# A windowed attention feeding a leaky feed-forward block: the weights' loads moved to directly behind the first values, and two casts moved between engines

## The chip, the cores and the metric

The kernel runs on one core of a Trainium2 chip. The core has a matrix engine (TensorE, PE in the profile), a vector engine (VectorE, DVE), an engine for functions of single elements (ScalarE, ACT), a general one (GpSimd, POOL) and one that only issues transfers here (SyncE, SP). Sixteen DMA engines move the data that SP and POOL ask for. The metric is the device time of one execution in microseconds (us), lower is better, as the median of several runs.

## The reference

`q`, `k` and `v` have 8 batches, 8 heads, 576 tokens and 64 channels per head. Every token attends to the tokens at most 32 places away:

```python
scores = (1 / sqrt(64)) * (q @ k.transpose(0, 1, 3, 2))
mask   = abs(pos[:, None] - pos[None, :]) <= 32
attn   = softmax(where(mask, scores, -1e9))
x      = (attn @ v).transpose(0, 2, 1, 3).reshape(4608, 512)
h      = x @ w_in                      # 512 -> 2048
out    = maximum(0.01 * h, h) @ w_out  # 2048 -> 512, float32
```

Inputs and outputs are float32. The kernel multiplies in bfloat16.

## The kernel before, in words

Heads go in pairs, four pairs to a batch; the two heads of a pair fill the 128 partitions. The first two batches (0 and 1) are treated in half sequences of 288 tokens, one "step" for each batch, half and pair; the later batches in blocks. For a step of batches 0 and 1 there are these pieces:

- `load_qk(b, p)` (L69) issues on SP one DMA for the queries and one for the keys of a pair, in float32. With `behind` given it has POOL first write one element of the target, so that SP's DMA waits until POOL comes to that place in its queue (L76).
- `load_cast_v(b, p)` (L137) issues on POOL two DMAs that load a pair's values and cast them on the way, into `vbd`.
- `cast_qk(b, p, q_eng, k_eng)` (L262) casts the loaded queries and keys to bfloat16, each on a given engine: VectorE or POOL by a copy (L270), ScalarE by an activation (L268). POOL is the default for both.
- `transposes(b)` (L299) is a generator. Each `next` issues the six PE transposes of one pair's queries or keys (L308) and the copy out of PSUM on ScalarE (L316 for queries, L322 for keys).
- `score(i)` (L398) does the score matmuls of step `i` into the one PSUM tile `ps` (L409 for batch 0, L416 for batch 1), the exponential on ScalarE (L421) and the product with the mask (L423), on POOL but for step 0.
- `sums(i)` (L436) sums the masked exponentials with a matmul of ones into the PSUM tile `s` (L447) and takes the reciprocal on VectorE (L452). The pool has one such tile, so the next `sums` waits for that reciprocal.
- `product(i)` (L455) multiplies with the values into the PSUM tile `x` (L463), and `scaled(i)` (L475) multiplies with the reciprocals into `xT` on VectorE (L477). There is one `x` tile as well.

The feed-forward block works on groups of tokens, 288 at first and 256 or 512 later: `h_mms` and `h_tile` (L498, L514) multiply with `w_in`, `o_tile` and `o_pair` (L562, L582) with `w_out`. Both weights stay on the chip as bfloat16. `load_w_in(f0, f1)` and `load_w_out(i)` (L653, L656) each issue on POOL one DMA of 512 KB that casts on the way; there are four of each.

The order of work is written out by hand: the tile framework runs with a manual schedule, and every engine executes its own instructions in the order of the program. Waits between engines, and the semaphores that signal a DMA's landing, are put in by the framework. The lines L660 to L781 hold the start: batch 0's transposes, steps 0 to 7, and the first two groups of the feed-forward block. Batch 1's queries and keys are loaded there (L718), and its transposes come inside group 1 (`second_pair`, L746). Behind that a planner spreads the remaining steps over the feed-forward matmuls by due times (L784 to L859); the change does not touch it.

`keep_busy(t, lo, n)` (L599) issues `n` matmuls of 224 columns whose results nobody reads, into part of a PSUM tile that is in use elsewhere (`ps` or a feed-forward tile).

Numbers of lines are those of the kernel before. In the kernel after, those from L599 to the start of the listing at L660 are 7 higher, and those behind the listing 6 higher.

Of the kernel before, what the change touches and what calls it, by code (L numbers as in the profile page):

```python
# [9 lines left out]
FP32 = mybir.dt.float32  # L10
# [6 lines left out]
def kernel(  # L17
# [15 lines left out]
    nc = tc.nc  # L33
# [7 lines left out]
    NPAIR = H // 2  # L41
# [19 lines left out]
    xps = ctx.enter_context(tc.tile_pool(name="xps", bufs=1, space=PS))  # L61
# [7 lines left out]
    def load_qk(b, p, behind=None):  # L69

        for into, src, name in ((qf, q, "qf"), (kf, k, "kf")):
            t = fload.tile([96, 2, RUN * D], FP32, name=f"{name}{p}")
            if behind is not None:
                behind.memset(t[0:1, 0, 0:1], 0.0)  # L76
                behind = None
            heads = src[b, 2 * p:2 * p + 2]
            if b < BY_DMA:
                nc.sync.dma_start(out=t, in_=heads.rearrange("a (p c) d -> p a (c d)", c=RUN))  # L80
            elif into is qf:
                nc.sync.dma_start(
                    out=t.rearrange("p a (g e) -> p a g e", g=3),
                    in_=heads.rearrange("a (g p c) d -> p a g (c d)", g=3, c=2),
                )
            else:
                nc.sync.dma_start(
                    out=t.rearrange("p a (c d) -> p a c d", d=D),
                    in_=heads.rearrange("a (c p) d -> p a c d", p=96),
                )  # L90
            into[b, p] = t
# [45 lines left out]
    def load_cast_v(b, p, heads=range(2)):  # L137

        for a in heads:
            r = slice(64 * a, 64 * a + 64)  # L140
            nc.gpsimd.dma_start(
                out=vbd[b % 2][r, p, :, r],
                in_=v[b, 2 * p + a].rearrange("(c p) d -> p c d", p=64),
            )
# [8 lines left out]
    ones_bd = const.tile([128, 128], BF16)  # L153
# [91 lines left out]
    ps = scps.tile([128, 1024], FP32)  # L245
# [16 lines left out]
    def cast_qk(b, p, q_eng=nc.gpsimd, k_eng=nc.gpsimd):  # L262
        for eng, src, dst in ((q_eng, qf, qb), (k_eng, kf, kb)):
            if eng is None:
                continue
            to, tok = dst[:, p], src[b, p].rearrange("p a (c d) -> p c a d", d=D)
            if eng is nc.scalar:
                eng.activation(out=to, in_=tok, func=AF.Copy)  # L268
            else:
                eng.tensor_copy(out=to, in_=tok)  # L270
# [74 lines left out]
    def where(i):  # L345
        return i // 8, (i // 4) % 2, i % 4
# [6 lines left out]
    def score_blocks(i):  # L353
        p, bs = i % NPAIR, blocks_of(i)
        n = 2 * 64 * len(bs)
        lo = 512 * (i % 2)
        sc = ps[:, lo:lo + n].rearrange("p (a w c i) -> p a w c i", a=2, c=2, i=32)
        for w, (b, m) in enumerate(bs):
            tok = qz[b % 2][:, p, m // 3].rearrange("p a (c i) -> p a c i", c=2)
            at = 32 * (m % 3)  # L360
            nc.tensor.matmul(  # L361
                sc[:, :, w], kz[b % 2][:, p, 64 * m:64 * m + 128],
                tok[:, :, :, at:at + 32], start=True, stop=True,
            )
        e = attn.tile([128, 2 * HALF], BF16, name="e")
        nc.scalar.activation(out=e[:, 0:n], in_=ps[:, lo:lo + n], func=AF.Exp, scale=scale)  # L366
        pr = prob[:, i % NPROB].rearrange("p n c i -> p (n c i)")[:, 0:n]
        nc.gpsimd.tensor_mul(pr, e[:, 0:n], band.rearrange("p w c i -> p (w c i)")[:, 0:n])  # L368
        probs[i] = pr.rearrange("p (a w i) -> p a w i", a=2, i=64)
# [28 lines left out]
    def score(i, masked_by=nc.gpsimd):  # L398
        if i >= OLD:
            return score_blocks(i)  # L400
        b, hf, p = where(i)
        by_c = qT[b][:, p].rearrange("p (c i) -> p c i", c=2)
        if b == 0:

            for a, n_, m in ((0, 0, 0), (1, 1, 0), (0, 0, 1), (1, 1, 1), (0, 0, 2),
                             (0, 1, 0), (1, 0, 0), (0, 1, 1), (1, 0, 1), (1, 0, 2)):
                blk, i0, n = WIN[hf][n_][m]
                r = slice(64 * a, 64 * a + 64)
                nc.tensor.matmul(  # L409
                    ps_v[r, n_, :, i0:i0 + n], first_keys[p][r, 64 * blk:64 * blk + 64],  # L410
                    by_c[r, :, hf * EVEN + i0:hf * EVEN + i0 + n], start=True, stop=True,
                )
        else:
            for n_, blocks in enumerate(WIN[hf]):
                for blk, i0, n in blocks:
                    nc.tensor.matmul(  # L416
                        ps_v[:, n_, :, i0:i0 + n], kbd[b % 2][:, p, blk],
                        by_c[:, :, hf * EVEN + i0:hf * EVEN + i0 + n], start=True, stop=True,
                    )
        e = attn.tile([128, 2 * HALF], BF16, name="e")  # L420
        nc.scalar.activation(out=e, in_=ps[:, P0:P0 + 2 * HALF], func=AF.Exp, scale=scale)  # L421
        pr = prob[:, i % NPROB]
        masked_by.tensor_mul(  # L423
            pr.rearrange("p n c i -> p (n c i)"), e, mask[hf].rearrange("p n c i -> p (n c i)"),
        )
        probs[i] = [pr, None, None]
# [9 lines left out]
    def sums(i):  # L436

        b, hf, p = where(i)
        pr, both, r = probs[i]
        if r is not None:  # L440
            return
        s = xps.tile([128, 512], FP32, name="s")[:, 0:HALF]
        if both is not None:
            nc.tensor.matmul(s, ones_bd, both, start=True, stop=True)  # L444
        else:
            for n in range(2):
                nc.tensor.matmul(  # L447
                    s, ones_bd, pr[:, n].rearrange("p c i -> p (c i)"),
                    start=(n == 0), stop=(n == 1),
                )  # L450
        r = recip.tile([128, HALF], FP32, name="r")
        nc.vector.reciprocal(r, s)  # L452
        probs[i][2] = r

    def product(i):  # L455

        b, hf, p = where(i)
        pr = probs[i][0]
        x = xps.tile([128, 512], FP32, name="x")[:, 0:HALF]
        x_v = x.rearrange("p (c i) -> p c i", c=2)  # L460
        parts = [(n_, *block) for n_ in range(2) for block in WIN[hf][n_]]
        for n_, blk, i0, n in parts:
            nc.tensor.matmul(  # L463
                x_v[:, :, i0:i0 + n], vbd[b % 2][:, p, blk, :], pr[:, n_, :, i0:i0 + n],
                start=(blk == parts[0][1]), stop=(blk == parts[-1][1]), skip_group_check=True,
            )
        probs[i][1] = x
# [7 lines left out]
    def scaled(i):  # L475
        _, x, r = probs.pop(i)
        nc.vector.tensor_mul(place(i), x, r)  # L477
# [15 lines left out]
    while t0 < new:  # L493
        n = 256 if t0 < 2048 else min(512, new - t0)
# [87 lines left out]
    def o_pair(hook):  # L582

        o = {}
        for j, part in ((0, 0), (0, 1), (0, 2), (1, 0), (1, 1), (1, 2), (0, 3), (1, 3)):
# [8 lines left out]
            if part == 3:  # L594
                o_sb = outp.tile([128, DMODEL], FP32, name="o_sb")
                nc.scalar.activation(out=o_sb, in_=o[j], func=AF.Copy)
                nc.sync.dma_start(out=out[ts(j, 128)], in_=o_sb)

    def keep_busy(t, lo, n):  # L599


        for _ in range(n):
            nc.tensor.matmul(
                t[:, lo:lo + 224], ones_bd, mask[0].rearrange("p n c i -> p (n c i)")[:, 0:224], start=False, stop=False,
                skip_group_check=True,
            )
# [46 lines left out]
    def load_w_in(f0, f1):  # L653
        nc.gpsimd.dma_start(out=w_in_bf[:, :, f0:f1], in_=w_in_r[:, :, f0:f1])

    def load_w_out(i):  # L656
        c = slice(4 * i, 4 * i + 4)
        nc.gpsimd.dma_start(out=w_out_bf[:, c, :], in_=w_out_r[:, c, :])
# [16 lines left out]
    next(first)  # L675
    next(first)
    load_cast_v(0, 3)
    cast_qk(0, 2, nc.vector)
    sums(0)
    score(1)  # L680
    load_w_in(0, 512)
    next(first)
    keep_busy(ps, 0, 2)
    next(first)
    keep_busy(ps, 0, 3)
    cast_qk(0, 3, nc.vector)
    score(2)
    sums(1)
    next(first)
    keep_busy(ps, 0, 3)  # L690
    next(first)
    product(0)
    scaled(0)
    load_w_in(512, 1024)
    sums(2)
    score(3)
    product(1)
    scaled(1)
    load_w_in(1024, 1536)
    keep_busy(ps, 0, 3)  # L700
    score(4)
    load_w_in(1536, 2048)
    h0 = h_first(0)
    h = next(h0)
    product(2)
# [3 lines left out]
    next(h0)  # L709
    score(5)  # L710
    next(h0)
    load_w_out(0)
    product(3)
    next(h0)
    scaled(3)
    load_w_out(1)

    for p in range(NPAIR):  # L718
        load_qk(1, p, nc.gpsimd if p == 0 else None)
    sums(4)  # L720
    next(h0)
    score(6)
# [71 lines left out]
    at, t = {1: 0.0}, 0.0  # L794
# [10 lines left out]
    t = at[2] - LEAD + 1.8  # L805
    while len(due) + 8 < NC:
# [3 lines left out]
        t = until  # L810
# [77 lines left out]
```

## Time and profile before

| | us |
|---|---|
| runs, median of 3 | 314.67 |
| runs, lowest and highest | 314.0, 315.95 |
| profiled execution | 315.61 |
| its span, first to last instruction | 313.9 |

| engine | busy, us |
|---|---|
| PE matmuls | 298.1 |
| PE weight loads (beside the matmuls) | 194.4 |
| VectorE (DVE) | 224.7 |
| POOL | 205.0 |
| ScalarE (ACT) | 202.2 |

The table's busy times are of one profiled execution; its span is what the views of the trace divide, and the profiled execution's own time is 1.7 us above it. In the rows of the trace, L12 is line 12 of the kernel, `out<-in` are the program's names of tiles, and `x6` is a count. A row of the timeline begins with its start and its length in us, and ends with the engine's idle time before it and what released it. A row of waits ends with the us in total, how often, and the longest. A row of the window table has the window, its length, then the busy us of PE, PE weight loads, DVE, ACT and POOL with counts, the granted clock of PE, the busy share of the DMA engines and their GB/s. A row of DMA issues has the size of one and the median us from issue to landing. A busy PE is not a PE at its peak: ends of matmuls are modelled.

### The profile page before, as it was taken

How to read it: one execution, taken by the hardware profiler on the slowest of the kernel's cores; microseconds unless marked ns; L12 is line 12 of the kernel's file. 1: busy time of each engine (PE TensorE's matmuls, PEld its weight loads, DVE VectorE, ACT ScalarE, POOL GpSimd, SP SyncE). 2: the span in 40 equal slices, each digit the busy share in tenths (PEclk: the TensorE clock that was granted, in tenths of full speed). 3: DMA queues.
4: the chain of work that ended last, by engine and by line, in shares of the span. 5: the costliest groups of instructions: out<-in, count | busy, mean ns of one | idle time of the engine just before them, and what ended most of it. 6: DMA issues, size and time to landing. Idle time of an engine off the chain costs nothing.

```text
span 313.9 us, 6723 instructions
## 1 busy us (share of the span) xinstructions
PE 298.1 (95%) x2511; PEld 194.4 (62%) x2540; DVE 224.7 (72%) x299; ACT 202.2 (64%) x418; POOL 205.0 (65%) x258
## 2 busy tenths in 40 slices
PE   2889979999999999999999999999999999999996
PEld 1567855476765858585858585858555555544643
DVE  6788668878669977898799776898679866753000
ACT  6537775274775858686858686767579548842731
POOL 8889789977799889589668357578947622110000
PEclk9999999999999999999999999999999999999999
DMA  7999999998999999989999994796970011011002
GB/s 198 180 166 172 268 250 132 240 187 168 209 219 201 138 277 184 203 173 255 183 186 179 255 199 90 143 230 156 196 137 2 15 68 55 0 36 67 33 25 79
DMA packets 122017, 48.29 MB, mean 154 GB/s; under 512 B 96256, under 2 KB 117504, under 8 KB 121984
## 3 DMA queue, kind: packets, MB, share of 16 engines
q1 hardware_dynamic: 108288, 42.48, 68.1%
q0 software_dynamic: 13696, 5.38, 14.6%
q8 instruction: 20, 0.33, 0.4%
q14 instruction: 13, 0.11, 0.1%
HBM read 36.70 MB, written 9.44 MB: 147 GB/s over the span
## 4 chain that ended last, share of the span: by engine, by line
PE 77%; DMA 10%; DVE 6%; POOL 3%; issue 2%; ACT 1%; SPq 0%; POOLq 0%; DVEq 0%; ACTq 0%
PE mm L574 34%; PE mm L501 33%; DMA kf<-in_k_dram 7%; DVE r L452 4%; PE ps L361 4%; PE s L379 2%; PE x L379 2%; DMA set<-kb 2%; POOL prob L368 1%; DMA set<-in_v_dram 1%; POOL kb L270 1%; PE s L447 1%; PE x L463 1%; DVE xT L477 1%; DVE r L388 1%
## 5 line engine op out<-in xcount | busy, mean ns | idle before, releaser
L501 PE MATMUL mm<-xT,w_in_bf 128*128 128x256 bf16 (+3 forms) x956 | 133.1, 294 | 0.3
L574 PE MATMUL mm<-w_out_bf,gT 128*128 128x512 bf16 (+2 forms) x537 | 122.5, 373 | 1.3
L388 DVE RECIPROCAL r<-r 128x256 f32<-128x256 f32 (+1 forms) x56 | 95.0, 1696 | 38.0 <-ACT r L387 37.5
L501 PEld LDWEIGHTS <-w_in_bf 128*128 128x128 bf16 x960 | 91.4, 98 | 30.2 <-issue 0.3
L368 POOL TENSOR_TENSOR prob<-e,band 128x512 bf16<-128x512 bf16 (+1 forms) x56 | 62.7, 1120 | 58.4 <-ACT e L366 57.2
L574 PEld LDWEIGHTS <-gT 128*128 128x128 bf16 x560 | 52.1, 98 | 54.1
L512 ACT ACTIVATE gT<-mm 128x288 bf16<-128x288 f32 (+2 forms) x112 | 50.2, 476 | 12.4 <-PE mm L501 9.5
L366 ACT ACTIVATE e<-ps 128x512 bf16<-128x512 f32 (+1 forms) x56 | 32.4, 579 | 27.8 <-PE ps L361 26.5
L579 ACT ACTIVATE o_sb<-mm 128x512 f32<-128x512 f32 (+2 forms) x35 | 20.5, 585 | 39.3 <-PE mm L574 39.1
L535 ACT ACTIVATE gT<-mm 128x512 bf16<-128x512 f32 x64 | 35.7, 596 | 5.5 <-PE mm L501 4.2
L452 DVE RECIPROCAL r<-s 128x288 f32<-128x288 f32 x16 | 31.2, 1952 | 4.4 <-PE s L444 2.3
L270 POOL CAST kb<-kf 96x768 bf16<-96x768 f32 x30 | 24.9, 830 | 3.6 <-DMA kf<-in_k_dram 3.2
L392 DVE TENSOR_TENSOR xT<-s,r 64x256 bf16<-64x256 f32 (+1 forms) x56 | 24.3, 434 | 3.6 <-PE ps L361 0.5
L392 DVE TENSOR_TENSOR xT<-x,r 64x256 bf16<-64x256 f32 (+1 forms) x56 | 24.4, 435 | 3.3
L361 PEld LDWEIGHTS <-set 128*128 128x128 bf16 x216 | 16.7, 98 | 9.7 <-DMA set<-kb 0.5
L423 POOL TENSOR_TENSOR prob<-e,mask 128x576 bf16<-128x576 bf16 x15 | 19.4, 1293 | 4.7 <-ACT e L421 4.6
L296 DVE COPY set<-kT 64x576 bf16<-64x576 bf16 x48 | 21.4, 446 | 1.2 <-DMA kT<-qb 0.3
L361 PE MATMUL ps<-set 128*128 128x128 bf16 x216 | 21.4, 219 | 0.3 <-DMA set<-kb 0.3
L275 POOL CAST set<-vbuf 128x640 bf16<-128x640 f32 x24 | 17.2, 718 | 3.8 <-DMA vbuf<-in_v_dram 3.8
L270 POOL CAST qb<-qf 96x768 bf16<-96x768 f32 x24 | 19.7, 820 | 0.0
L379 PEld LDWEIGHTS <-set 128*128 128x128 bf16 x432 | 18.0, 98 | 0.5
L421 ACT ACTIVATE e<-ps 128x576 bf16<-128x576 f32 x16 | 10.4, 651 | 10.2 <-PE ps L409 6.1
(83 smaller groups left out, 241.3 us busy)
## 6 DMA issues: line engine op xcount, KB each, us to landing
qf<-in_q_dram SPq DMA_DIRECT2D x32, 288.0 KB, 5.8
kf<-in_k_dram SPq DMA_DIRECT2D x32, 288.0 KB, 6.3
out_dram<-o_sb SPq DMA_DIRECT2D x35, 256.0 KB, 3.0
vbuf<-in_v_dram SPq DMA_DIRECT2D x15, 256.0 KB, 4.8
w_in_bf<-in_moe_w_in_dram POOLq DMA_DIRECT2D x4, 512.0 KB, 5.7
w_out_bf<-in_moe_w_out_dram POOLq DMA_DIRECT2D x4, 512.0 KB, 14.9
vbuf<-in_v_dram SPq DMA_DIRECT2D x10, 192.0 KB, 4.6
set<-in_v_dram POOLq DMA_DIRECT2D x16, 72.0 KB, 7.0
```

What stands on the lines that cost most here:

```text
L270: eng.tensor_copy(out=to, in_=tok)
L361: nc.tensor.matmul(sc[:, :, w], kz[b % 2][:, p, 64 * m:64 * m + 128], tok[:, :, :, at:at + 32], start=True, stop=True,)
L366: nc.scalar.activation(out=e[:, 0:n], in_=ps[:, lo:lo + n], func=AF.Exp, scale=scale)
L368: nc.gpsimd.tensor_mul(pr, e[:, 0:n], band.rearrange("p w c i -> p (w c i)")[:, 0:n])
L379: nc.tensor.matmul(x[:, a, w], vw[b % 2][:, p, m, a:a + 2].rearrange("p n d -> p (n d)"), pr[:, a, w], start=True, stop=True,)
L388: nc.vector.reciprocal(r[:, 0:n], r[:, 0:n])
L392: nc.vector.tensor_mul(xT[rows, p, t0:t0 + n].rearrange("p (w i c) -> p w c i", i=32, c=2), x[rows, a].rearrange("p (w c i) -> p w c i", c ...
L452: nc.vector.reciprocal(r, s)
L501: nc.tensor.matmul(h[:, 0:n], w_in_bf[:, c, ts(f, 128)], xT[:, c, t0:t0 + n], start=(c == 0), stop=(c == DMC - 1),)
L512: nc.scalar.activation(out=to, in_=h, func=AF.Prelu, alpha=0.01)
L535: nc.scalar.activation(out=gT[:, f - 1:f + 1, t0:t0 + 256], in_=hh.rearrange("p (f t) -> p f t", f=2), func=AF.Prelu, alpha=0.01,)
L574: nc.tensor.matmul(o[:, lo:hi], gT[:, f, t0:t0 + 128], w_out_bf[:, f, lo:hi], start=(f == 0), stop=(f == FFC - 1),)
```

## The change

The weights' loads move ahead in POOL's queue. The first two chunks of `w_in` are issued directly behind batch 0's values, ahead of the mask product of step 1; the third and the fourth follow the products of steps 2 and 3, and `w_out`'s first chunk the product of step 4. Batch 1's queries and keys are loaded ahead of `w_out`'s second chunk, and not behind it. Pair 2's keys are cast on VectorE where POOL cast them; pair 3's queries on ScalarE where VectorE cast them. Three of the `keep_busy` calls become `warm_up` calls: nine matmuls of 128 columns in all for eight of 224, into a PSUM tile of their own (the pool of `x`) and not into `ps`.

```diff
+    def warm_up(n):
+        t = xps.tile([128, 512], FP32, name="x")
+        for _ in range(n):
+            nc.tensor.matmul(
+                t[:, 0:128], ones_bd, ones_bd, start=True, stop=True, skip_group_check=True,
+            )
...
     load_cast_v(0, 3)
-    cast_qk(0, 2, nc.vector)
+    load_w_in(0, 512)
+    load_w_in(512, 1024)
+    cast_qk(0, 2, nc.vector, nc.vector)
     sums(0)
     score(1)
-    load_w_in(0, 512)
     next(first)
-    keep_busy(ps, 0, 2)
+    warm_up(2)
     next(first)
-    keep_busy(ps, 0, 3)
-    cast_qk(0, 3, nc.vector)
+    cast_qk(0, 3, nc.scalar)
+    warm_up(4)
     score(2)
+    load_w_in(1024, 1536)
     sums(1)
     next(first)
-    keep_busy(ps, 0, 3)
+    warm_up(3)
     next(first)
     product(0)
     scaled(0)
-    load_w_in(512, 1024)
     sums(2)
     score(3)
+    load_w_in(1536, 2048)
     product(1)
     scaled(1)
-    load_w_in(1024, 1536)
     keep_busy(ps, 0, 3)
     score(4)
-    load_w_in(1536, 2048)
+    load_w_out(0)
     h0 = h_first(0)
...
     score(5)
     next(h0)
-    load_w_out(0)
+    for p in range(NPAIR):
+        load_qk(1, p, nc.gpsimd if p == 0 else None)
+    load_w_out(1)
     product(3)
     next(h0)
     scaled(3)
-    load_w_out(1)
-
-    for p in range(NPAIR):
-        load_qk(1, p, nc.gpsimd if p == 0 else None)
     sums(4)
```

## The prediction

> **What bounds the kernel now.** I read the page's totals first, then what TensorE (PE) waited for, then the stages.
>
> ```profile
> span 313.9 us, 6723 instructions
> PE 298.1 (95%) x2511; PEld 194.4 (62%) x2540; DVE 224.7 (72%) x299; ACT 202.2 (64%) x418; POOL 205.0 (65%) x258
> ...
> PE tp L308 <- POOL kb L270: 1.9, 2, 1.1
> PE s L447 <- DVE r L452: 1.0, 3, 0.6
> PE ps L361 <- DMA set<-kb: 0.3, 1, 0.3
> ...
> 40.00:45.00 5.00, 3.18 (x40) 2.63 (x41) 2.98 (x7) 3.77 (x9) 4.69 (x7) 1.00 1.17 271
> 50.00:55.00 5.00, 4.80 (x39) 2.66 (x38) 4.75 (x10) 2.68 (x6) 5.00 (x8) 1.00 0.96 143
> 55.00:60.00 5.00, 4.39 (x36) 2.28 (x35) 4.79 (x5) 1.02 (x3) 4.87 (x7) 1.00 1.33 212
> 60.00:70.00 10.00, 9.95 (x87) 7.03 (x86) 6.67 (x10) 6.27 (x15) 7.70 (x10) 1.00 1.21 214
> ```
>
> PE is busy 95% of the span. In the window rows PE's busy time is the second figure: from 60 us on it leaves nothing to speak of (9.95 of 10, and from there to the end one semaphore wait, the 0.3 of L361). So whatever this change does before 60 us passes through to the end as PE's arrival time there, and only two stretches hold idle PE that an edit could win back: 40 to 45 us (1.8 us idle; the two waits of L308 for POOL's cast of keys, 1.9 us) and 50 to 60 us (0.2 + 0.6 us, for DVE's reciprocals). The two together are 2.7 us, under 1% of the span. What comes before 20 us is a chain of single steps that starts the work, and any delay in it moves PE's whole queue.
>
> **POOL's queue, where the weights move to.** The weights' DMAs are issued by POOL, between its own work, in program order.
>
> ```profile
> 4.10 6.21 POOL L141 DMA_DIRECT2D set<-in_v_dram  x8
> 10.63 0.82 POOL L270 CAST kb<-kf 96x768 bf16<-96x768 f32 x1 [0.33 <-DMA kf<-in_k_dram]
> 12.07 1.27 POOL L423 TENSOR_TENSOR prob<-e,mask 128x576 bf16<-128x576 bf16 x1 [0.62 <-ACT e L421]
> 13.51 0.83 POOL L654 DMA_DIRECT2D w_in_bf<-in_moe_w_in_dram  x1 [0.17 <-issue]
> 14.34 0.84 POOL L270 CAST kb<-kf 96x768 bf16<-96x768 f32 x1
> ...
> set<-in_v_dram POOLq DMA_DIRECT2D x1, 72.0 KB, 9.1
> ```
>
> The last row is the first of the eight value loads, taken alone: issued at 4.10, landed 9.1 us later, at 13.2. This matters because in the compiled program POOL's DMAs take eight semaphores in rotation: the ninth, which is the first weights' load, carries a wait for the first value load, the tenth for the second, in both kernels. Before, that wait is free: POOL gets there at 13.51, after its cast and its mask product. After, the two loads stand right behind the eight value loads, so POOL reaches them at 4.10 + 6.21 = 10.31 and waits until 13.2. Queued behind the waiting issue are the mask product of step 1 and the key cast of pair 3. So: issue 13.3, two issues of 0.83 each to 14.95; product of step 1 from 14.95 to 16.2 (before 12.07 to 13.34, **2.9 us later**); cast of pair 3's keys to 17.05 (before 15.18); product of step 2, again 1.27, to 18.3. The DMA queue itself gains little at its head, since the value loads hold it anyway; the second chunk does start earlier, but no wait of PE for a weight is in the list above for it to shorten.
>
> **Who waits for it.** PE takes its instructions in order.
>
> ```profile
> 14.38 0.66 PE L447 MATMUL s<-prob,ones_bd 128*128 128x288 bf16 x2
> 15.08 1.96 DVE L452 RECIPROCAL r<-s 128x288 f32<-128x288 f32 x1 [1.33 <-PE s L447]
> 17.10 0.42 PE L447 MATMUL s<-prob,ones_bd 128*128 128x288 bf16 x2 [0.20 <-DVE r L452]
> 17.55 1.96 DVE L452 RECIPROCAL r<-s 128x288 f32<-128x288 f32 x1 [0.16 <-PE s L447]
> 19.43 0.40 DVE L477 TENSOR_TENSOR xT<-x,r 128x288 bf16<-128x288 f32 x1
> 19.88 0.40 PE L463 MATMUL x<-prob,set 128*128 128x96 bf16 x5 [0.38 <-DVE xT L477]
> 20.84 0.65 PE L501 MATMUL mm<-xT,w_in_bf 128*128 128x288 bf16 x4
> ```
>
> sums(1) (14.38) needs the product of step 1, so it starts at 16.25; its reciprocal at 16.95 instead of 15.08, to 18.9; sums(2) at 19.0 instead of 17.10, and at the slow 0.66 (below) instead of 0.42, so the next reciprocal starts at 19.65 instead of 17.55; scaled(1), product(2) and the first matmul of the feed-forward follow at 21.6, 22.05 and 23.0. **Loss in front: 2.15 us.**
>
> **The casts and the warm-up.**
>
> ```profile
> 12.28 1.48 DVE L270 CAST qb<-qf 96x768 bf16<-96x768 f32 x1
> 13.09 0.65 ACT L322 ACTIVATE kT<-tp 128x576 bf16<-128x576 bf16 x1 [0.52 <-PE tp L308]
> 14.50 0.65 ACT L421 ACTIVATE e<-ps 128x576 bf16<-128x576 f32 x1 [0.77 <-PE ps L409]
> 12.04 0.53 PE L603 MATMUL ps<-mask,ones_bd 128*128 128x224 bf16 x2 [0.16 <-ACT e L421]
> 9.45 0.55 DVE L270 CAST qb<-qf 96x768 bf16<-96x768 f32 x1
> ```
>
> Pair 2's keys go to DVE, which is free from 10.0 to 10.40: at the 0.55 of the cast at 9.45, from the landing at 10.6 to 11.2. The new warm-up writes another PSUM tile, so it doesn't wait for the exponential as the row at 12.04 does; the transposes behind it start near 11.9 instead of after both fillers, 12.4. Pair 3's queries go to ACT: no ACT cast of 96x768 is in the trace, between the 0.65 of 576 columns and the 1.48 that DVE needed; I take 0.85, by the nearer row. It falls into the 0.77 us for which ACT waited before 14.50 anyway. All this wins up to 0.5 us ahead of sums(1) and hands it to PE's wait for POOL: I count it as nothing. Were the stall not there, the cover would be gone and the 0.3 to 0.5 us would count. The 1.48 leaving DVE count nothing either: the reciprocal behind it waited 1.33 us for PE.
>
> **PE's slow start.**
>
> ```profile
> 9.22 0.66 PE L308 MATMUL tp<-ident,kb 96*128 96x96 bf16 x6 [0.80 <-DVE kb L270]
> ...
> PEclk9999999999999999999999999999999999999999
> ```
>
> The page's row of the granted clock reads full from the start and doesn't show it, but the two matmuls of sums(1) take 0.66 at 14.38 and those of sums(2) 0.42 at 17.10, so PE turned fast in between. Before that it had worked since this row's 9.22 with no pause above 0.3 us. In the changed kernel this work is cut by the stall: PE stands from about 13.95 to 16.25, and again near 18.5 and 20.5. Gapless work starts at 22.05. Bounds for the cost: nothing, if PE turns fast by then; at the other end, slow for as long as 9.22 to 16.6 (7.4 us) counted from 22.05, to 29.5, so 6.5 us of feed-forward at about half speed, 3.2 us. I take 0.9, nearer to nothing, since the last, unbroken part of before (13.79 to 16.6) was under 3 us: slow to about 24.8, half of 1.8 us. **PE comes to batch 1's transposes 2.15 + 0.9 = 3.05 us later.**
>
> By the Trainium skill, "TensorE: Matmul & The Clock Gate", Part 1 (the HAM clock gate), the clock opens after about 3.4 us of sustained work, in a free-running window, and an idle window closes it. By that rule the stall starts the count afresh; worst case two windows from 22.05, to 28.9, which would put about 2.9 in place of 0.9, an estimate. The trace agrees in the slow first matmuls; it doesn't show the window.
>
> **Batch 1's queries and keys.**
>
> ```profile
> 25.58 0.09 POOL L76 MEMSET qf<- 1x1 f32 x1
> 25.70 0.31 SPq L80 DMA_DIRECT2D qf<-in_q_dram  x1
> 24.05 1.55 POOL L658 DMA_DIRECT2D w_out_bf<-in_moe_w_out_dram  x2
> w_out_bf<-in_moe_w_out_dram POOLq DMA_DIRECT2D x4, 512.0 KB, 14.9
> 46.08 2.75 PE L590 MATMUL mm<-w_out_bf,gT 128*128 128x512 bf16 x12
> qf<-in_q_dram SPq DMA_DIRECT2D x1, 288.0 KB, 8.8
> qf<-in_q_dram SPq DMA_DIRECT2D x32, 288.0 KB, 5.8
> 40.10 0.82 POOL L270 CAST kb<-kf 96x768 bf16<-96x768 f32 x1 [2.28 <-DMA kf<-in_k_dram]
> 40.98 0.43 PE L308 MATMUL tp<-ident,kb 96*128 96x96 bf16 x6 [1.06 <-POOL kb L270]
> 43.84 0.82 POOL L270 CAST kb<-kf 96x768 bf16<-96x768 f32 x1 [0.21 <-DMA kf<-in_k_dram]
> 44.71 0.43 PE L308 MATMUL tp<-ident,kb 96*128 96x96 bf16 x6 [0.84 <-POOL kb L270]
> ```
>
> SP starts these eight loads after POOL's memset and has nothing else to issue in this stretch. The memset is now one weights' issue (0.8) earlier in POOL's queue; but POOL's product ahead of it follows PE and is 2 to 3 us late, and with the other reorderings I place it near 26.4, 0.8 later than 25.58. In exchange only one chunk of w_out stands ahead, and w_in's second and third are through sooner. The first load took 8.8 us against a median of 5.8 over all: up to 3 us of it was queueing. So landings move by +0.8 to -2.2 us; I take 0, as a shared DMA moves the same bytes. The second chunk of w_out, now issued behind the memset at about 26.5 instead of 24.9, lands some 15 us later by the row, at 41.5, and PE reads it from 46: nothing. Then the casts end at 40.92 and 44.66 as now, and PE, which without its waits would come to the second at 44.71 - 1.9 = 42.8, comes at 42.8 + 3.05 = 45.85. The 1.9 us of waits swallow most of the loss; left is 1.15. Of the 0.8 idle at 50 to 60, DVE's chain behind the last query load stands where it was, so PE gets that back too: left is +0.35.
>
> **Sum:** 2.15 + 0.9 - 1.9 - 0.8 = +0.35 us. The profiled execution took 315.61 (span 313.9 and 1.7 around it), so it would take 316.0; the runs' median is 314.67, 0.94 lower, so I forecast **315.1**, no change.
>
> **Rivals.**
> - The wait hides after all, and the early loads do their work (POOL's stall covered, or value loads landing by 10.3). Against it: 13.2 from the rows above. Then 0.3 in front, 1.5 to 1.9 at 40 to 45, up to 0.8 behind: -2.3, so **312.4**. Chance 0.15.
> - The slower side: PE stays slow through the first feed-forward group because the stall breaks its work. Price 3.2 in place of 0.9; it decides once the loss in front passes 1.9 + 0.8 = 2.7. Sum 2.15 + 3.2 - 2.7 = +2.65: **317.3**. For it: three pauses where there were none. The rule of the Trainium skill named above speaks for it too. Against: dense work from 22 on. Chance 0.15.
> - The change doesn't bring the loads sooner but later (+0.8): the second cast ends at 45.5, DVE's chain and PE with it, and nothing is regained behind: +0.8 to 1.2, **315.7**. Chance 0.2.
> - The loads land 1 to 2 us sooner with PE fast by 23: 2.15 - 2.7 = -0.55: **314.1**. Chance 0.15.
>
> **How the numbers follow.** The forecast has 0.35. Range 312.8 to 317.4: it holds the forecast and its neighbours, most of the slower rival, and a part of the fast one. The measurement tells about 1% (3.1 us) from no change; the three runs alone lie 314.0 to 315.95. A gain above that would need more than all the idle PE that the stages hold (2.7): 0.03. A loss above it needs the slow PE and late loads together: 0.07. Same: 0.90.
>
> **What would show it.** POOL idle from about 10.3 to 13.3, ended by a DMA or "issue", ahead of the first weights' load; sums(1) near 16.2 instead of 14.38; the first feed-forward matmul near 23.0; PE's waits of 1.06 and 0.84 gone at 41 and 45; PE's idle before the reciprocals at 50 to 57 smaller. I am wrong if POOL doesn't stall at 10.3, if the slow matmuls last beyond 25, or if the second key cast ends before 43.5 or after 45.5.

## The result, and the profile after

The changed kernel takes 316.19 us (median; 315.01 to 318.24), the kernel before 314.69 in the same series. The ratio is 1.0052, with a 95% interval of 1.0036 to 1.0067: slower by 1.5 us, inside the 1% that was forecast as no change, and 1.1 us above the forecast of 315.1. The profiled execution took 315.80 with a span of 314.1, so the two profiles alone differ by 0.2 us of span.

The page of the changed kernel, its totals; then the waits of PE over the whole span and of POOL from 5 to 60 us (us in total, times, longest):

```profile
span 314.1 us, 6755 instructions
PE 300.7 (96%) x2541; PEld 195.7 (62%) x2541; DVE 228.3 (73%) x299; ACT 202.2 (64%) x419; POOL 204.7 (65%) x257
...
PE s L447 <- POOL prob L423: 2.2, 1, 2.2
PE s L447 <- DVE r L452: 0.8, 3, 0.3
...
POOL w_in_bf L661 <- DMA set<-in_v_dram: 2.5, 1, 2.5
```

The last row is the wait that the change adds: POOL stands 2.5 us at the first weights' load, until the values' DMA lands. The first row of waits is its price on PE: sums(1) waits 2.2 us for POOL's mask product. PE's two waits for key casts, 1.9 us before, are gone from the list but for a rest too short to show. (The counts of matmuls differ between the two pages because a few records are missing from the first.)

Two rows of the kernel before for comparison, batch 1's first transposes and the `sums` near 56 us:

```profile
36.91 0.42 PE L308 MATMUL tp<-ident,qb 96*128 96x96 bf16 x6
56.10 0.42 PE L447 MATMUL s<-prob,ones_bd 128*128 128x288 bf16 x2 [0.61 <-DVE r L452]
```

The timeline of the changed kernel in the front, then at batch 1's casts and transposes:

```profile
10.04 0.78 DVE L270 CAST kb<-kf 96x768 bf16<-96x768 f32 x1
12.81 0.83 ACT L268 ACTIVATE qb<-qf 96x768 bf16<-96x768 f32 x1
12.89 1.53 POOL L661 DMA_DIRECT2D w_in_bf<-in_moe_w_in_dram  x2 [2.46 <-DMA set<-in_v_dram]
14.49 1.27 POOL L423 TENSOR_TENSOR prob<-e,mask 128x576 bf16<-128x576 bf16 x1
15.81 0.64 PE L447 MATMUL s<-prob,ones_bd 128*128 128x288 bf16 x2 [2.18 <-POOL prob L423]
18.50 0.66 PE L447 MATMUL s<-prob,ones_bd 128*128 128x288 bf16 x2 [0.32 <-DVE r L452]
23.17 0.69 PE L447 MATMUL s<-prob,ones_bd 128*128 128x288 bf16 x2
23.65 0.98 PE L501 MATMUL mm<-xT,w_in_bf 128*128 128x288 bf16 x4
24.56 0.43 PE L409 MATMUL ps<-set,kT 64*64 64x64 bf16 x10
27.06 0.09 POOL L76 MEMSET qf<- 1x1 f32 x1
...
32.80 6.05 POOL L750 MEMSET set<- 128x1152 bf16 x6
40.00 0.42 PE L308 MATMUL tp<-ident,qb 96*128 96x96 bf16 x6
44.78 0.84 POOL L270 CAST kb<-kf 96x768 bf16<-96x768 f32 x1
45.68 0.43 PE L308 MATMUL tp<-ident,kb 96*128 96x96 bf16 x6
56.30 0.42 PE L447 MATMUL s<-prob,ones_bd 128*128 128x288 bf16 x2 [0.23 <-DVE r L452]
```

sums(1) moves from 14.38 to 15.81, sums(2) from 17.10 to 18.50. The two matmuls of a `sums` still take 0.69 at 23.17, and the ten of a score 0.43 at 24.56: PE turns fast only there (at 24.3 by the record of the granted clock in the trace), where it was fast at 17.10 before. The first feed-forward matmul starts at 23.65 (before 20.84), batch 1's first transposes at 40.00 (before 36.91), the transposes behind the second of the key casts at 45.68 (before 44.71), and the `sums` of 56.10 stands at 56.30. So 3.1 us of loss in front are 1.0 us at 45 and 0.2 at 56.

The same in the window table of the changed kernel (PE's busy time is the second figure):

```profile
40.00:45.00 5.00, 5.00 (x62) 4.25 (x60) 4.13 (x9) 4.85 (x13) 4.88 (x8) 1.00 1.20 264
50.00:55.00 5.00, 5.00 (x51) 3.06 (x49) 4.73 (x10) 2.67 (x5) 5.00 (x7) 1.00 0.71 121
55.00:60.00 5.00, 4.77 (x38) 2.43 (x36) 4.79 (x5) 1.56 (x3) 4.87 (x8) 1.00 1.38 215
```

PE's 1.8 us of idle at 40 to 45 are filled, and 0.6 of the 0.8 at 50 to 60. The late PE has used up the slack that the late loads had made, in this pair of profiles.

### The profile page after: what moved, and what is told of

Its sections match the earlier page's. It is cut to its first block, busy times and chain, and to the rows that moved or that the text cites. A ratio compares the mean times of both kernels' runs of the same rounds, so it can differ in the third digit from the quotient of the medians.

```text
span 314.1 us, 6755 instructions
## 1 busy us (share of the span) xinstructions
PE 300.7 (96%) x2541; PEld 195.7 (62%) x2541; DVE 228.3 (73%) x299; ACT 202.2 (64%) x419; POOL 204.7 (65%) x257
## 4 chain that ended last, share of the span: by engine, by line
PE 77%; POOL 11%; DMA 4%; DVE 3%; issue 2%; ACT 2%; SPq 0%; POOLq 0%; ACTq 0%; DVEq 0%
PE mm L574 34%; PE mm L501 33%; PE ps L361 3%; DVE r L452 2%; POOL set L750 2%; PE x L379 2%; PE s L379 2%; POOL kb L270 2%; POOL prob L368 2%; DMA set<-kb 1%; DMA kf<-in_k_dram 1%; POOL prob L423 1%; POOL qb L270 1%; POOL set L141 1%; PE s L447 1%
## 5 line engine op out<-in xcount | busy, mean ns | idle before, releaser
L574 PE MATMUL mm<-w_out_bf,gT 128*128 128x512 bf16 (+2 forms) x560 | 124.6, 373 | 0.0
L392 DVE TENSOR_TENSOR xT<-s,r 64x256 bf16<-64x256 f32 (+1 forms) x56 | 24.3, 434 | 3.6 <-PE ps L361 0.5
L392 DVE TENSOR_TENSOR xT<-x,r 64x256 bf16<-64x256 f32 (+1 forms) x56 | 24.3, 435 | 3.3
L270 POOL CAST kb<-kf 96x768 bf16<-96x768 f32 x29 | 24.3, 838 | 1.4 <-DMA kf<-in_k_dram 0.9
L361 PEld LDWEIGHTS <-set 128*128 128x128 bf16 x216 | 16.8, 98 | 9.7 <-DMA set<-kb 0.4
```

Source lines behind the costliest of these rows:

```text
L361: nc.tensor.matmul(sc[:, :, w], kz[b % 2][:, p, 64 * m:64 * m + 128], tok[:, :, :, at:at + 32], start=True, stop=True,)
L392: nc.vector.tensor_mul(xT[rows, p, t0:t0 + n].rearrange("p (w i c) -> p w c i", i=32, c=2), x[rows, a].rearrange("p (w c i) -> p w c i", c ...
L574: nc.tensor.matmul(o[:, lo:hi], gT[:, f, t0:t0 + 128], w_out_bf[:, f, lo:hi], start=(f == 0), stop=(f == FFC - 1),)
```

## The experiments

The theory at the start: POOL's wait for the first value load delays the mask product of step 1 and with it PE's whole queue; the slow clock adds to it; the waits for key casts and reciprocals give most of it back. The rivals: the shorter fillers and the cast on ScalarE cost the time; or early weights take DMA time from what is needed first.

### The weights back in their places

```diff
 # the changed kernel, with
-    load_w_in(0, 512)        # behind load_cast_v(0, 3)
-    load_w_in(512, 1024)
+    load_w_in(0, 512)        # behind score(1)
+    load_w_in(512, 1024)     # behind scaled(0); the others as before, too
```

> The changed kernel with the six loads of w_in and of w_out's first chunk put back to their places in POOL's queue of before; the casts, the fillers and the order of batch 1's loads stay as changed. Stall theory (the loss comes from POOL waiting at the first weights' load for the first value load to land): POOL's idle of 2.46 us before that load falls below 0.5 us, sums(1) starts near 13.8 instead of 15.8, the first feed-forward matmul near 20.4 instead of 23.65, the two waits for key casts at 41 and 45 us come back in part; time 313.5 to 314.5, 1.7 to 2.7 below the changed kernel. Rival (the fillers of 128 columns and the cast on ScalarE make PE slow for longer): the time stays at 315.5 to 316.5 with the turn of the clock near 24.

Measured: 314.33 us; ratio to the kernel before 0.999 (0.997 to 1.001), against 1.0052 for the whole change. PE's timeline in this kernel:

```profile
13.39 0.66 PE L447 MATMUL s<-prob,ones_bd 128*128 128x288 bf16 x2
20.74 0.65 PE L501 MATMUL mm<-xT,w_in_bf 128*128 128x288 bf16 x4
42.77 0.43 PE L308 MATMUL tp<-ident,kb 96*128 96x96 bf16 x6 [0.35 <-POOL kb L270]
```

sums(1) no longer waits for POOL, and the loss is gone: the weights' places are worth 1.9 us. The rival with the fillers isn't out altogether: sums(1) starts 0.2 to 1.0 us earlier than in three profiles of the kernel before (14.38, 14.15, 13.57), and yet the first feed-forward matmul starts no earlier than there (20.84, 20.60, 20.26). PE's clock turned at 20.2 (by the record of the granted clock) and not at 16.4 to 16.8.

### The same early places, without the wait

```diff
 # the changed kernel, with
-    load_cast_v(0, 3)        # ahead of load_w_in(0, 512)
     load_w_in(0, 512)
     load_w_in(512, 1024)
...
     score(2)
+    load_cast_v(0, 3)
     load_w_in(1024, 1536)
```

> The changed kernel with pair 3's two value loads put behind the mask product of step 2, so that the first two weights' loads are the seventh and eighth DMA of POOL and take semaphores that are free; they stand even earlier in the queue. Stall theory: no wait of POOL before the first weights' load, sums(1) near 13.8, first feed-forward matmul near 20.4, time 312.5 to 314. Rival (early weights themselves cost, by taking DMA time from the values and from batch 1's queries and keys): POOL does not wait, but the time stays above 315.5, with PE waiting for values or for key casts.

Measured: 313.70 us; ratio 0.9971 (0.9948 to 0.9994). POOL's first weights' loads, and PE's first feed-forward matmul:

```profile
8.75 1.55 POOL L661 DMA_DIRECT2D w_in_bf<-in_moe_w_in_dram  x2
21.76 1.04 PE L501 MATMUL mm<-xT,w_in_bf 128*128 128x288 bf16 x4
```

The two loads go out 4 us earlier than in the changed kernel and POOL doesn't wait, though they stand two value loads further ahead. Early weights do no harm; the wait does. It comes from the semaphores: these are now POOL's seventh and eighth DMA, and in the trace they take the last two of POOL's eight semaphores; in the changed kernel they take the first two a second time. The expected start of the feed-forward block near 20.4 was missed by 1.4 us: PE stayed slow to 22.5, with no stall in front of it.

### The stall filled

```diff
 # the changed kernel, with
     score(2)
+    warm_up(20)
     load_w_in(1024, 1536)
     sums(1)
```

> The changed kernel with 20 more filler matmuls of 128 columns ahead of sums(1), about 2 us of PE work in the place where PE waits 2.2 us for POOL. The stall stays. If the slow clock is the second part of the loss, PE turns fast before 20 us instead of at 24.3, the first feed-forward matmul starts near 22.8 instead of 23.65, and the time falls by 0.5 to 1.2 us, to 315.0 to 315.7. If the clock's turn costs nothing that reaches the end, the time stays at 316.2 (plus or minus 0.4).

Measured: 314.77 us; ratio 1.000 (0.998 to 1.002), 1.4 us below the changed kernel. PE in this kernel:

```profile
15.88 0.64 PE L447 MATMUL s<-prob,ones_bd 128*128 128x288 bf16 x2 [0.31 <-POOL prob L423]
18.58 0.42 PE L447 MATMUL s<-prob,ones_bd 128*128 128x288 bf16 x2 [0.90 <-DVE r L452]
22.32 0.65 PE L501 MATMUL mm<-xT,w_in_bf 128*128 128x288 bf16 x4
38.39 0.42 PE L308 MATMUL tp<-ident,qb 96*128 96x96 bf16 x6
```

POOL waits as long as in the changed kernel (2.4 us) and sums(1) starts as late, 15.88 against 15.81. But PE is fast from 16.9, the feed-forward block starts 1.3 us earlier and batch 1's first transposes 1.6 us (38.39 for 40.00), and the kernel is as fast as the one before, 0.2 us below the expected range. So the slow clock behind the stall is worth 1.4 us. That doesn't make the wait itself free: PE still comes to batch 1's transposes 1.5 us later than before (38.39 for 36.91), which the waits for key casts give back (0.2 us is left of 1.9). A kernel without the stall and with a fast PE comes to 312.58 (below).

### The first two loads alone

```diff
 # the kernel before, with
     load_cast_v(0, 3)
+    load_w_in(0, 512)
+    load_w_in(512, 1024)
...
     score(1)
-    load_w_in(0, 512)
...
     scaled(0)
-    load_w_in(512, 1024)
```

> The kernel before with one edit: the first two loads of w_in directly behind the values, all casts, fillers and other loads as before. Stall theory: the cast of pair 2's keys stands behind the waiting load on POOL too, so its transposes start near 15.5 instead of 12.4 and the loss in front is larger than that of the whole change, 3.5 to 5 us at the first feed-forward matmul; the waits at 41 and 45 us give back about 1.9 and those behind 50 about 0.5; time 316 to 317.5. Rival (the weights' places do nothing, the loss is that of the other edits): 314.7, as before.

Measured: 317.90 us; ratio 1.0113 (1.0085 to 1.0142). POOL's wait and PE's wait behind it:

```profile
13.29 1.52 POOL L654 DMA_DIRECT2D w_in_bf<-in_moe_w_in_dram  x2 [2.88 <-DMA set<-in_v_dram]
15.73 0.66 PE L308 MATMUL tp<-ident,kb 96*128 96x96 bf16 x6 [3.16 <-POOL kb L270]
24.18 0.65 PE L501 MATMUL mm<-xT,w_in_bf 128*128 128x288 bf16 x4
47.22 0.43 PE L308 MATMUL tp<-ident,kb 96*128 96x96 bf16 x6 [1.09 <-POOL kb L270]
```

It lies 0.4 above the expected range. The front is nearly as expected: pair 2's key cast stands behind POOL's wait, and the first feed-forward matmul is 3.3 us later, where 3.5 to 5 was expected. The clock turned at 19.9, ahead of the feed-forward block, so this loss is the stall's and the late keys', without a slow feed-forward. The waits for batch 1's keys don't give it back, because the weights that follow move POOL's memset, and the key loads behind it, to 28.9: PE waits at 47 again. In the whole change two other edits would soften the first: the cast on VectorE takes the keys out of POOL's queue, and the loads' new place ahead of a weights' issue keeps them from going as late (the memset at 27.06).

### Batch 1's loads alone

```diff
 # the kernel before, with
     load_w_out(0)
+    for p in range(NPAIR):
+        load_qk(1, p, nc.gpsimd if p == 0 else None)
+    load_w_out(1)
     product(3)
     next(h0)
     scaled(3)
-    load_w_out(1)
-
-    for p in range(NPAIR):
-        load_qk(1, p, nc.gpsimd if p == 0 else None)
```

> The kernel before with one edit: batch 1's queries and keys issued ahead of w_out's second chunk. If this part does something by itself, SP's first load starts 0.8 us earlier (near 24.9), PE's two waits for key casts (1.06 and 0.84 us) shrink together by 0.8 to 1.6 us and the time falls by as much less what the reciprocals at 50 to 57 us set: 313.7 to 314.4. If a shared DMA only deals the same bytes out in another order, the waits stay within 0.4 us of 1.9 and the time is 314.7.

Measured: 313.77 us; ratio 0.9967 (0.9951 to 0.9982): this part alone is faster by 1.0 us. POOL's memset, the landing of batch 1's four key loads (the last figure is the median us from issue to landing), batch 1's first transposes, the cast that waits for a key load, and PE's one wait for a key cast:

```profile
25.34 0.09 POOL L76 MEMSET qf<- 1x1 f32 x1
...
kf<-in_k_dram SPq DMA_DIRECT2D x4, 288.0 KB, 12.2
...
37.45 0.42 PE L308 MATMUL tp<-ident,qb 96*128 96x96 bf16 x6
39.21 0.82 POOL L270 CAST kb<-kf 96x768 bf16<-96x768 f32 x1 [0.78 <-DMA kf<-in_k_dram]
43.81 0.43 PE L308 MATMUL tp<-ident,kb 96*128 96x96 bf16 x6 [0.75 <-POOL kb L270]
```

Of 1.9 us of waits 0.75 are left. The memset isn't 0.8 earlier as expected (25.34 against 25.58), and with one chunk of weights less ahead the keys land 12.2 us after they are issued, against 14.2 and 13.3 in the first two profiles of the kernel before. But the cast that waits for them starts at 39.21, and in three profiles of the kernel before at 40.10, 39.20 and 39.75. Against the second of these nothing is gained at the transposes behind the second key cast (43.80 there, behind a wait of 0.83), and PE waits less here also because it comes later (37.45 for 36.91, 36.68 and 36.34). That this part is faster is shown by the times, and the second branch of the expectation, a time of 314.7, is out; by which way it gains, this one profile doesn't show.

### A fast PE from the start

The 38 fillers fill PE's idle time up to 11 us. They were put into the kernel before, into the changed kernel and into that with the values last.

```diff
     load_cast_v(0, 1)
+    warm_up(16)
     next(first)
     next(first)
+    warm_up(8)
...
     score(0, masked_by=nc.vector)
+    warm_up(3)
     next(first)
+    warm_up(8)
     next(first)
...
     sums(0)
+    warm_up(3)
     score(1)
```

> The kernel before with 38 more filler matmuls of 128 columns in the places where PE idles before 11 us (16 ahead of the first transposes, then 8, 3, 8 and 3). If PE's slow start is a matter of its own activity, PE turns fast before 11 us instead of at 16.6, the first feed-forward matmul starts 0.5 to 1.5 us earlier than 20.84, and the time falls less than that, by 0 to 0.8 us, to 313.9 to 314.7, since the key casts at 41 and 45 us then hold PE.

> The changed kernel with the same 38 fillers. The stall of POOL stays (2.4 us); what PE's slow clock adds to it is taken away. If the median's loss of 1.5 us is the clock's, this kernel comes to 314.0 to 315.0, at most 0.5 above the kernel before with the same fillers. If it is the stall's own, it stays 1.2 or more above that kernel, at 315.5 or more.

> The kernel with pair 3's value loads put last (no stall) and the same 38 fillers: a fast PE from 11 us on and no wait of POOL. Theory: first feed-forward matmul near 19.5 to 20, time 312.0 to 313.3, below both kernels. Rival (whatever is won in front is held again by batch 1's key casts at 41 and 45): PE waits there again by 1 us or more and the time stays at 313.7 or above.

Measured: the kernel before with them 314.45 us, ratio 0.9979 (0.9960 to 0.9999); the changed kernel with them 315.82, ratio 1.0029 (1.0012 to 1.0046); the values last with them **312.58, ratio 0.9920 (0.9903 to 0.9937)**, below both kernels, and 1.1 below the same kernel without the fillers. The clock turned at 11.8, 9.9 and 14.0. What I expected of the front didn't come: the first feed-forward matmul starts at 20.64 in the kernel before with fillers (0.5 to 1.5 earlier than 20.84 was expected) and at 20.86 with the values last (19.5 to 20).

The changed kernel stays 1.4 us above the kernel before with the same fillers, which I had put down as the mark of a stall that costs by itself. The trace shows that it can't be read so: the fillers didn't take the slow clock away. The window table of the changed kernel with fillers (PE's busy time is the second figure, the granted clock the third from the end):

```profile
9.90:13.20 3.30, 2.20 (x41) 1.73 (x39) 2.80 (x3) 2.37 (x6) 0.88 (x2) 1.00 1.92 188
13.20:16.60 3.40, 1.31 (x24) 1.10 (x25) 0.44 (x1) 1.49 (x4) 3.33 (x5) 1.00 1.84 168
16.70:20.00 3.30, 2.60 (x28) 1.60 (x25) 2.86 (x3) 1.48 (x3) 1.73 (x2) 0.50 1.23 201
20.00:23.40 3.40, 3.16 (x26) 2.27 (x26) 1.60 (x3) 0.84 (x2) 3.03 (x3) 0.50 1.08 155
23.60:27.00 3.40, 3.26 (x43) 2.13 (x41) 3.29 (x3) 1.19 (x3) 2.56 (x5) 1.00 1.24 157
```

PE is fast from 9.9. In the stretch of the stall it works 1.31 of 3.4 us, and from 16.7 on it is granted half the clock, to 23.4: longer than the stall lasted, and nearly as late as in the changed kernel without fillers (24.3). So the stall closes the clock anew, though PE was fast before. It isn't this execution alone: in all twelve the mean granted clock of the span is 0.984 to 0.989, and two stretches of 3.4 us at half speed make 0.989. The Trainium skill, "TensorE: Matmul & The Clock Gate", Part 1, gives a free-running window of about 3.4 us, after which a busy PE is granted the full clock and an idle one half. The stretches agree with that length (6.8 us at half speed here, 3.4 below); the closing here needed no idle window, a pause of 2.0 us in one was enough.

The kernel before with fillers shows the same at another place, in its window table:

```profile
42.00:45.90 3.90, 1.90 (x21) 1.25 (x20) 1.47 (x4) 2.18 (x5) 2.59 (x5) 1.00 1.23 253
46.00:49.30 3.30, 3.30 (x14) 1.34 (x12) 3.04 (x5) 1.81 (x2) 3.30 (x5) 0.50 1.93 132
49.40:52.00 2.60, 2.60 (x24) 1.49 (x22) 2.19 (x8) 0.92 (x2) 2.60 (x5) 1.00 0.16 29
```

PE didn't wait for the first of the key casts, came to the second one earlier (42.38 where it came at 43.45), waited 1.9 us for it, and ran the next 3.4 us at half speed. What was won was not only held up at the cast, it was paid for with clock. In this kernel that is the exception: of its eleven executions two have a mean granted clock under 0.999, 0.995 for this one and 0.989, and they are the two longest (315.73 and 315.68; the others 313.11 to 314.97).

With the values last and the loads ahead neither pause is there, and PE is fast from 14 on:

```profile
20.86 0.65 PE L501 MATMUL mm<-xT,w_in_bf 128*128 128x288 bf16 x4
24.42 0.09 POOL L76 MEMSET qf<- 1x1 f32 x1
36.96 0.42 PE L308 MATMUL tp<-ident,qb 96*128 96x96 bf16 x6
42.64 0.43 PE L308 MATMUL tp<-ident,kb 96*128 96x96 bf16 x6
```

The feed-forward block and batch 1's first transposes stand where they stood before (20.84, 36.91). The gain is made behind: POOL comes to the memset 1.2 us earlier, the keys are cast in time, and the transposes behind the second key cast stand at 42.64 for 44.71.

### More profiles of both kernels

> The kernel before once more, for a second profile. Its first profiled execution took 315.61, 0.9 above the median of its runs. If the turn of PE's clock differs from one execution to the next and makes that difference, this one turns at another time than 16.6, or falls back to the slow clock behind the waits at 41 and 45 us, and its span follows: about half a us of span for each us of slow clock that falls into the feed-forward stage. If the turn stays at 16.6 within 0.5 and the span still differs by 0.8 or more, the spread has another cause.

> As the second profile of the kernel before: a third sample of the turn of PE's clock, of the two waits for key casts near 41 and 45 us, and of the span. Spans without a slow stretch in the feed-forward stage should lie at 312.5 to 313.3.

> The changed kernel once more. Its first profile turned at 24.3, had its first feed-forward matmul at 23.65 and a span of 314.1, below the median of its runs less 1.7 (314.5). The stall is fixed by the values' landing, so POOL's wait of 2.2 to 2.6 us and sums(1) near 15.8 should be the same; what differs is the turn of the clock (17 to 28) and with it the first feed-forward matmul (23 to 24.5) and the span (313.5 to 316.5).

> As the second profile of the changed kernel: a third sample of the turn of PE's clock and of the span. If the stall sends PE back to the slow clock each time, no sample turns for good before 19.5, and the mean span of the three lies 1 to 2 us above that of the three of the kernel before.

Measured: the kernel before 314.47 and 314.80, spans 312.8 and 313.1; the changed kernel 315.68 and 315.38, spans 313.9 and 313.7. With the first profiles the spans average 313.25 before and 313.91 after: 0.66 apart, where 1 to 2 was expected. The clock turned at 16.4 and 16.8 before (first profile 16.6), and at 23.6 and 24.8 after (first 24.3): it isn't the turn that made the first profile of the kernel before the longest of the three. POOL's wait in the changed kernel was 2.98 and 2.22 us (2.2 to 2.6 expected), and in the first of these two sums(1) started at 16.24. PE's timeline of the second profile of the kernel before, and POOL's first weights' load in it:

```profile
13.68 0.83 POOL L654 DMA_DIRECT2D w_in_bf<-in_moe_w_in_dram  x1 [0.57 <-DMA set<-in_v_dram]
40.08 0.43 PE L308 MATMUL tp<-ident,kb 96*128 96x96 bf16 x6 [0.51 <-POOL kb L270]
43.80 0.43 PE L308 MATMUL tp<-ident,kb 96*128 96x96 bf16 x6 [0.83 <-POOL kb L270]
```

The two key transposes stand 0.9 us earlier than the 40.98 and 44.71 of the profile that the prediction was made from; in the third profile they stand between, at 40.63 and 44.34. In the first, batch 1's keys had landed late. Its waits for key casts (1.9 us in all) are not larger than in the others (1.3 and 2.1), but its PE stands latest at the `sums` of 56.10 (55.19 and 55.74). The first row shows, in the kernel before, the very wait that the prediction took from the list of semaphores: this time POOL reached the load 0.57 us before the value load had landed.

## Why the prediction was right, and where it was off

- **POOL's wait.** Right: it stood from 10.43 (8.93 + 1.50, the end of the value loads' issue) to 12.89 where 10.3 to 13.3 was forecast, named as a wait for the value load. The mask product stood at 14.49 (forecast 14.95), sums(1) at 15.81 (16.25).
- **The casts and fillers.** Right to cost nothing beside the stall: ScalarE took 0.83 (I took 0.85), VectorE 0.78 (0.55). That the new fillers are weaker than the old I hadn't weighed; in the two kernels with the new ones and without the stall the clock turned at 20.2 and 22.5, and behind a stall it turned at 19.9 with the old ones (the first two loads alone) and at 23.6 to 24.8 with the new. Whether the fillers or the windows' place made that, no run here separates. By the time, casts and fillers together are what the kernel with the weights back (0.999) and that with batch 1's loads alone (0.9967) differ in: 0.2%, with intervals that overlap.
- **The slow clock.** Mechanism right, size wrong. The term was 0.9 us, for feed-forward work at half speed to 24.8; the clock turned at 24.3. With the stall filled PE came to batch 1's transposes at 38.39 instead of 40.00: 1.6 us for the slow clock. I left out that the steps between the stall and the feed-forward block go at half speed as well. By the time, filling the stall is worth 1.4 us.
- **Front in sum.** 3.05 us later at batch 1's transposes was forecast, 3.09 measured, and that is luck: the slow clock took 1.6 where I had 0.9, the rest of the front 1.5 (38.39 against 36.91, with the stall filled) where I had 2.15.
- **The loads.** Their issue came at 27.06 where 26.4 was forecast. No landing decided: the second key cast, at 44.78, started behind POOL's own queue (memsets to 38.85, two casts, value loads, a memset) with no idle time. Forecast for the transposes behind it: 45.85; measured 45.68. But I had left the casts where they were, the second one to 44.66; it ends at 45.62 (45.55 and 45.43 in the two other profiles), past the 45.5 that I had named as a sign of being wrong in two of the three. It costs little only because PE comes about as late.
- **What comes back.** 1.9 us at 40 to 45 and 0.8 at 50 to 60 were forecast, from 3.05 to 0.35; measured from 3.09 to 0.2. In the pair of profiles the sum held. What I named for the second part, the chain behind the last query load, isn't what the chain of work that ended last goes through in these two: that is a value load of batch 1, which landed at 49.36 before and 49.56 after.
- **From the profile to the median: here the forecast was off.** It was 316.0 for the profiled execution of the changed kernel, which took 315.80. I then took 0.94 us off, since the profiled execution of the kernel before stood that much above the median, as if both kernels shared it. They don't: the changed kernel's stood 0.39 below its median. In the kernel before it came at least in part from keys whose casts started 0.4 to 0.9 us later than in the two other profiles, and the changed kernel has that slack eaten by its late PE. Against the second profile, with 42.5 for PE's arrival without its waits (43.80 less the 1.3), the same working gives 45.55 and about +1.0 us at the end: 313.8 by its span of 312.8. Against the third (44.34 and 2.1) it gives about +0.2, 313.3 by its span of 313.1. The three spans after are 313.7 to 314.1.
- **What stays open.** The medians differ by 1.5 us and the mean spans of three profiles by 0.66, so more than half of the loss is seen in no profile. None of the profiled executions is one of the longest of the changed kernel (up to 318.24). A clock that closes again later isn't the reason: the mean granted clock is 0.999 or 1.000 in all 22 executions.
- **The rivals.** "The change doesn't bring the loads sooner but later" is nearest by the time (315.7) and had the end of the second cast right (45.5), though POOL's queue made it and not a landing, and PE did regain most of it behind. "The clock stays slow" had the right mechanism at twice its price (3.2 for 1.6). "The wait hides" is out. "The loads land sooner" is borne out for the loads alone only by the time (1.0 us); here POOL's queue came in its place.

## What to carry to other kernels

Before a DMA is moved forward in an engine's queue, count which semaphore it takes: the ninth of a queue that has eight waits for the first to land, and everything behind it on that engine waits too; two loads put behind instead of ahead cured it here. A pause of PE can cost its length and the clock behind it, so a hole that can't be closed is worth filling with idle matmuls (1.4 us here). And a place read from one profile is that execution's: the kernel before stood 0.9 us apart at 56 us in two of its profiles, so take two or three before slack is booked as a cover.

## What the runs showed that was not expected

One pause of about 2 us can be enough to halve PE's clock for a stretch of 3.4 us or two, in the middle of dense work as well: 46.0 to 49.3 behind a wait of 1.9 us, 16.7 to 23.4 behind one of 2.0. Opening takes more than closing: the stretch of 16.7 to 20.0 with 2.60 of 3.3 us busy was followed by another slow one, that of 20.0 to 23.4 with 3.16 of 3.4 by a fast one. Cut into stretches of 3.4 us from the turn of the clock, the other traces with a clock record fit up to 60 us: PE was busy for 1.4 us in the two stretches that closed it and for 2.0 or more in all that kept it open, and it opened behind none under about 3.1, though twice not behind 3.2.
